# Output products of 24 heads by seven block products, with the row of softmax sums sent through DRAM

## The chip, the cores and the metric

The kernel runs on one core of a Trainium2 chip. The metric is the device time of one execution in microseconds (us), the median of several runs. The engines have separate, in-order instruction queues: TensorE (PE; its weight loads are listed as PEld), VectorE (DVE), ScalarE (ACT) and GpSimd (POOL); SyncE (SP) issues nearly all transfers, in order as well.

## The reference

A transformer block on x of 2048 rows by 576, float32. Six vectors for shift, gain and gate come from a condition vector c.

```python
h = layernorm(x) * (1 + ca) + sa
q = (h @ wq)                          # 32 heads of 128
k, v = the last 512 rows of the caches, 16 heads, each for two heads of q
o = softmax(q k^T / sqrt(128)) @ v
x = x + ga * (o @ wo)                 # wo: 4096 x 576
h = layernorm(x) * (1 + cb) + sb
x = x + gb * ((silu(h @ w1) * (h @ w3)) @ w2)   # 576 -> 4608 -> 576
```

## The kernel before

Every matmul runs in float32r on operands split into a high and a low half (`split`: ACT casts the high half, VectorE or POOL subtracts it from the source), three matmuls for one product.

**Attention.** The 2048 rows are four blocks of 512, whose residual sums stand in SBUF in `acc[0]` to `acc[3]`. The first half of attention does blocks 0 and 1, the second blocks 2 and 3. A *slot* is one head with one block: 64 slots in each half, 0 to 63 and 64 to 127; apart from each half's first four, the two blocks of a head follow each other. A slot has four *steps*, t = 0 to 3, for 128 rows each. In step t of iteration i of the main loop TensorE turns the probabilities of slot i-1 (`turn`), makes the scores of slot i (`scores`), a part of the queries of slot i+1 (`query`), and the product of the heads' output of slot i-2 with wo (`attend_out`, `back`). After the fourth step come the products with V of slot i-1 (`values`). `attend_out` is six matmuls of 128 by 288 columns into one PSUM pair, E, from which VectorE scales by one over the softmax sum, a value per row, and adds to `acc`.

**Around it.** While attention runs, the MLP's weights are made ready: `make_set` forms, for 128 columns of w1 and w3, seven combined blocks (Strassen's way of doing a product of 2 by 2 blocks with seven block products), and `make_rows` does the same for 256 rows of w2 (`make_rows` with -1 prepares, then seven pieces follow). POOL makes sums and low halves, ACT the high halves, SP stores each piece to DRAM and later loads it. In the second half, h of blocks 0 and 1 is normalized (`norm`), stored, and combined likewise (`combine`, three chunks of seven steps). All these are small tasks in a table, placed by `at(i, t, task, ...)` and called by `run(i, t)` at the end of step t of iteration i (`("m", g)` stands for group g of the MLP). The place in the program sets the place in every engine's queue. `early`, `late` and `items` hand out the places of the weights' tasks: pieces are made in slots 10 to 56 and 66 to 74 at 1.25 a step, and in 85 to 116 at 0.82.

**The MLP** runs its down product by seven block products already (`down`, `multiply`, `finish`): a unit is two jobs of three matmuls into one PSUM pair, two blocks of 512 rows need 14 units for 256 rows of weights, against 16 by plain products.

Tiles rotate in pools of fixed size: `w` (8), `xn` (4), `hf` (2), `ah` and `al` (3), `o` (3), `hs` (7). A write waits for the last reader of the tile that stood there.

## Time and profile before

| | |
|---|---|
| median of 3 runs | 3063.23 us (3062.53 to 3064.26) |
| the profiled execution | 3066.29 us, span 3064.5 us |
| granted TensorE clock, mean | 0.996 |
| bytes | read 369.8 MB, written 150.2 MB |
| maxima and exponentials (DVE L319, ACT L325), 512 each | 683 and 690 ns |

Slot 24 begins at 382 us, slot 97 at 1403 us, and attention ends at some 1820 us. The page gives, for each engine, its busy time and share of the span, and the chain of work that ended last. A query in windows gives the busy time in a stretch. A row of instructions reads: line, engine, operation, result<-operands, shape and count | busy us, mean ns of one | idle time ahead of it and what ended it. The chain's rows are start us, duration us, engine, tile, line, count.

### The profile page before, as it was taken

The numbers are of one execution on the slowest core, as the hardware profiler recorded it, in microseconds if no ns is written. First come the engines' busy times: TensorE is split into PE (matmuls) and PEld (weight loads), VectorE is DVE, ScalarE is ACT, GpSimd is POOL, SyncE is SP. The second block draws the span as 40 slices with busy tenths as digits, with TensorE's granted clock in tenths as the row PEclk, the third lists the DMA queues.
The fourth block names the chain that finished last, engine by engine and source line by source line (L and its number), as shares of the span: only waits on it lengthen the run. The fifth ranks groups of instructions, "written<-read, shape, count | busy, mean of one in ns | idle before, by whom it ended". The sixth has DMA issues, their size and how long they took to land.

```text
span 3064.5 us, 47936 instructions
## 1 busy us (share of the span) xinstructions
PE 3027.4 (99%) x16948; PEld 2654.4 (87%) x16948; DVE 2002.5 (65%) x3042; ACT 1481.7 (48%) x3107; POOL 1635.3 (53%) x1656
## 2 busy tenths in 40 slices
PE   7999999999999999999999999999999999999998
PEld 6888888888888888888888888888888888888887
DVE  6776676777777777777777766555555555555555
ACT  4556666666666665666665553333333222322222
POOL 3257887888734731667775103346555463443444
PEclk8999999999999999999999999999999999999999
DMA  4235546555512532354544135667666766666664
GB/s 143 76 130 191 184 163 198 182 184 184 179 42 76 181 101 65 127 183 168 160 163 149 40 141 187 210 219 259 240 229 219 279 238 193 203 200 203 199 197 141
DMA packets 330128, 523.13 MB, mean 171 GB/s; under 512 B 32800, under 2 KB 161824, under 8 KB 328096
## 3 DMA queue, kind: packets, MB, share of 16 engines
q1 hardware_dynamic: 329280, 520.06, 51.5%
q8 instruction: 135, 2.21, 0.3%
q14 instruction: 105, 0.86, 0.1%
q10 hardware_dynamic: 608, 0.00, 0.0%
HBM read 369.76 MB, written 150.18 MB: 170 GB/s over the span
## 4 chain that ended last, share of the span: by engine, by line
PE 94%; DVE 2%; POOL 2%; ACT 1%; issue 1%; DMA 1%; SPq 0%; ACTq 0%; POOLq 0%; DVEq 0%
PE py L577 15%; PE pe L282 13%; PE px L577 11%; PE pq L266 11%; PE pt L335 7%; PE pf L653 6%; PE pe L653 6%; PE po L353 4%; PE po L352 4%; PE po L351 4%; PE pss L317 4%; PE pss L315 4%; PE pss L316 4%; PE pq L274 2%; PE pt L252 0%
## 5 line engine op out<-in xcount | busy, mean ns | idle before, releaser
L325 ACT ACTIVATE p<-pss,nm 128x512 f32<-128x512 f32 x512 | 353.3, 690 | 367.4 <-DVE nm L319 367.1
L577 PE MATMUL py<-hset,wset 128*128 128x512 f32 x2016 | 506.9, 391 | 0.0
L366 DVE SCALAR_TENSOR_TENSOR acc<-pe,r,acc 128x576 f32<-128x576 f32 x512 | 416.8, 814 | 53.6 <-PE pe L282 47.9
L319 DVE TENSOR_REDUCE nm<-pss 128x1 f32<-128x512 f32 x512 | 349.7, 683 | 118.2 <-PE pss L317 118.0
L577 PEld LDWEIGHTS py<-hset,wset 128*128 128x128 f32 x2016 | 362.6, 188 | 58.9
L577 PE MATMUL px<-hset,wset 128*128 128x512 f32 x1512 | 380.1, 391 | 0.0
L282 PEld LDWEIGHTS pe<-o,oth 128*128 128x128 f32 x2048 | 326.7, 188 | 48.7 <-DVE acc L366 6.1
L342 DVE TENSOR_TENSOR ptl<-pt,pth 128x512 fp32r<-128x512 f32 x512 | 349.0, 682 | 16.1 <-ACT pth L336 15.6
L282 PE MATMUL pe<-o,oth 128*128 128x288 f32 x2048 | 355.8, 296 | 2.7 <-DVE acc L366 2.6
L336 ACT CAST pth<-pt 128x512 fp32r<-128x512 f32 x512 | 301.1, 588 | 37.1 <-PE pt L335 33.3
L577 PEld LDWEIGHTS px<-hset,wset 128*128 128x128 f32 x1512 | 275.6, 188 | 49.4
L335 PE MATMUL pt<-ident,p 128*128 128x128 f32 x2048 | 307.7, 273 | 4.6 <-DVE ptl L342 2.6
L85 POOL TENSOR_TENSOR akv<-u,akv 128x512 fp32r<-128x512 f32 x141 | 182.1, 1302 | 237.8 <-ACT akv L84 236.3
L335 PEld LDWEIGHTS pt<-ident,p 128*128 128x128 f32 x2048 | 249.8, 141 | 18.6 <-issue 3.0
L315 PE MATMUL pss<-kh,qh 128*128 128x512 f32 x512 | 244.9, 478 | 0.7 <-ACT qh L84 0.7
L85 DVE TENSOR_TENSOR otl<-po,oth 128x512 fp32r<-128x512 f32 x128 | 88.6, 692 | 225.8 <-ACT oth L84 225.8
L497 POOL TENSOR_TENSOR wmade<-wraw,wmade 128x256 fp32r<-128x256 f32 x252 | 186.6, 740 | 80.5 <-ACT wmade L496 62.0
L282 PE MATMUL pe<-o,otl 128*128 128x288 f32 x1024 | 219.0, 295 | 0.0
L84 ACT CAST oth<-po 128x512 fp32r<-128x512 f32 x128 | 75.1, 587 | 295.6 <-PE po L353 295.6
L317 PE MATMUL pss<-kh,ql 128*128 128x512 f32 x512 | 202.9, 396 | 0.0
L316 PE MATMUL pss<-kl,qh 128*128 128x512 f32 x512 | 202.6, 396 | 0.0
L353 PE MATMUL po<-ptl,vh 128*128 128x512 f32 x512 | 201.1, 393 | 1.2 <-DVE ptl L342 1.2
(181 smaller groups left out, 6522.7 us busy)
## 6 DMA issues: line engine op xcount, KB each, us to landing
oset<-od SPq DMA_DIRECT2D x106, 576.0 KB, 4.8
od<-omade SPq DMA_DIRECT2D x133, 288.0 KB, 2.7
oraw<-in_A_wo SPq DMA_DIRECT2D x64, 288.0 KB, 3.1
wraw<-in_B_w SPq DMA_DIRECT2D x144, 128.0 KB, 2.7
wraw<-in_A_wq SPq DMA_DIRECT2D x64, 256.0 KB, 3.2
w2raw<-in_B_w SPq DMA_DIRECT2D x38, 288.0 KB, 3.6
oset<-od SPq DMA_DIRECT2D x35, 288.0 KB, 3.3
wraw<-in_B_w SPq DMA_DIRECT2D x288, 32.0 KB, 2.1
```

Source lines behind the costliest of these rows:

```text
L266: nc.tensor.matmul(ps, (wh if k < 2 else wl)[:, m, :], hT[DC + m if k == 1 else m], start=s == 0, stop=False,)
L282: nc.tensor.matmul(E[:, h, :HALF], a[:, rows], b[:, h * HALF : (h + 1) * HALF], start=n == 0, stop=n == 2)
L315: nc.tensor.matmul(pss, st["qh"][:, rows], kh, start=True, stop=False)
L316: nc.tensor.matmul(pss, st["qh"][:, rows], kl, start=False, stop=False)
L317: nc.tensor.matmul(pss, st["ql"][:, rows], kh, start=False, stop=True)
L319: nc.vector.tensor_reduce(nm, pss, axis=AX.X, op=ALU.max, negate=True)
L325: nc.scalar.activation(p, pss, AF.Exp, bias=nm, accum_out=st["l"][:, t : t + 1])
L335: nc.tensor.transpose(ps[:, j, :], p[:, j * P : (j + 1) * P], ident)
L342: nc.vector.tensor_sub(pt[1][:, :, cols], state[i]["t"], pt[0][:, :, cols].bitcast(F32))
L366: nc.vector.scalar_tensor_tensor(a, E[:, :, :HALF], st["r"][:, t : t + 1], a, op0=ALU.mult, op1=ALU.add)
L577: nc.tensor.matmul(ps, w[:, a, :], h[:, b, :], start=start and n == 0, stop=stop and n == 6, skip_group_check=True)
L653: nc.tensor.matmul(ps[:, h, :HALF], a[:, rows], w[:, b, :], start=m == 0, stop=m == 2)
```

## The change

For slots 72 to 119 (`FAST`, twelve groups of four slots; a group is two heads and blocks 2 and 3) the output products are made by seven block products:

- `values` no longer splits po. VectorE multiplies po by one over the softmax sums, laid out along the columns of each partition, into a block in SBUF (`blocks`). For that the 128 by 4 sums of a slot are inverted (`invert`), stored to DRAM as they lie, and loaded into all partitions in the next slot (`spread`); the multiplication reads them in turned order.
- POOL makes four sums of the group's four blocks (`out_sum`: s3, s1, s2, s4), and seven blocks are split (`out_split`): p7 and p2 with the low half on POOL, p4, p6, p1, p5 and p3 with it on VectorE.
- 14 units (`out_unit`) take the place of 16, one in a step, called ahead of the other tasks of a step. VectorE adds each to `acc[2]`, `acc[3]` or to sums that stand where `acc[0]` and `acc[1]` were; these two are moved to DRAM in slots 68 to 71 and back at the end (`move_x`). `finish_out` and `finish_out_first` add the sums up in slots 125 to 127.
- The pieces of wo for these heads are made by `make_rows` with the gate "a" and go through DRAM like those of w2. The weights' tasks are handed out anew: 33 sets or pairs of rows in slots 10 to 56, the rest and the twelve new pairs evenly over slots 66 to 116.
- h of blocks 0 and 1 is normalized four slots earlier, and combined two steps in a slot, beginning in slots 82, 87 and 92 (before: 86, 94 and 102, one step in a slot). Between slot 71 and that combining's last steps the pieces use only the tiles `w`.
- The heads of slots 120 to 123 get wo twice, plain and turned for block 3 (`put_turned`), since `acc[3]` holds combined sums then.

TensorE, second half, one step and what follows it. Before, in the last step (pe is bank E):

```order
L274 MATMUL pq<-hT,wl 128x512
L282 MATMUL pe<-o,oth 128x288 x4
L282 MATMUL pe<-o,otl 128x288 x2
L351 MATMUL po<-pth,vh 128x512
L352 MATMUL po<-pth,vl 128x512
```

Now, in the step of slot 77 that holds the second new unit (oah and oal are the halves of a split block, oset the loaded pieces of wo):

```order
L275 MATMUL pq<-hT,wl 128x512
L721 MATMUL pe<-oset,oah 128x288 x2
L721 MATMUL pe<-oset,oal 128x288
L721 MATMUL pe<-oset,oah 128x288 x2
L721 MATMUL pe<-oset,oal 128x288
L355 MATMUL po<-pth,vh 128x512
```

A unit is still six matmuls; it stands in 14 of 16 steps.

VectorE, one slot of the second half. Before (nm are the maxima, ptl the low halves of the turned probabilities, acc the sums out of bank E, ql and otl low halves of queries and outputs):

```order
L319 TENSOR_REDUCE nm<-pss 128x1
L342 TENSOR_TENSOR ptl<-pt,pth 128x4x128
L366 SCALAR_TENSOR_TENSOR acc_86<-pe,r,acc_86 128x576
L319 TENSOR_REDUCE nm<-pss 128x1
L342 TENSOR_TENSOR ptl<-pt,pth 128x4x128
L85 TENSOR_TENSOR ql<-pq,qh 128x512
L366 SCALAR_TENSOR_TENSOR acc_86<-pe,r,acc_86 128x576
L85 TENSOR_TENSOR otl<-po,oth 128x512
L358 RECIPROCAL r<-l 128x4
```

Now, steps 1 to 3 of slot 78, for the first group (os are the blocks, oal their low halves; acc_83 is `acc[0]`, where sums and the row of sums stand; in this first group sums are copied, later added):

```order
L85 TENSOR_TENSOR oal<-os,oah 128x512
L323 TENSOR_REDUCE nm<-pss 128x1
L346 TENSOR_TENSOR ptl<-pt,pth 128x4x128
L694 COPY acc_83<-pe 128x576
L85 TENSOR_TENSOR oal<-os,oah 128x512
L323 TENSOR_REDUCE nm<-pss 128x1
L346 TENSOR_TENSOR ptl<-pt,pth 128x4x128
L85 TENSOR_TENSOR ql<-pq,qh 128x512
L694 COPY acc_83<-pe 128x576
L377 RECIPROCAL r<-l 128x4
L360 TENSOR_TENSOR os<-po,acc_83 128x512
```

The low halves of p1 and p5 stand between the sums and the next maxima, and the product of po with the row of sums stands where the low half of the output was.

POOL, slots 78 to 81 or so. Before, gates, splits of wo, wq and V:

```order
L779 TENSOR_TENSOR oraw<-oraw,gate_a 128x576
L85 TENSOR_TENSOR o<-oraw,o 128x576
L85 TENSOR_TENSOR wl<-wraw,wh 128x640
L779 TENSOR_TENSOR oraw<-oraw,gate_a 128x576
L85 TENSOR_TENSOR vl<-kvraw,vh 128x512
```

Now, in slot 81, from the sums of a set of w1 and w3 to s2 (the last row):

```order
L515 TENSOR_TENSOR wraw<-wraw 128x384
L516 TENSOR_TENSOR wraw<-wraw 128x384
L519 TENSOR_TENSOR wmade<-wraw,wmade 128x256
L520 TENSOR_TENSOR wmade<-wraw,wmade 64x128
L519 TENSOR_TENSOR wmade<-wraw,wmade 128x256
L520 TENSOR_TENSOR wmade<-wraw,wmade 64x128
L574 TENSOR_TENSOR w2raw<-w2raw,gate_a 128x576 x2
L575 TENSOR_TENSOR w2raw<-w2raw 128x288
L576 TENSOR_TENSOR w2raw<-w2raw 128x288
L577 TENSOR_TENSOR w2raw<-w2raw 128x288
L579 TENSOR_TENSOR w2raw<-w2raw 128x288
L706 TENSOR_TENSOR os<-os 128x512
```

Pieces and a preparation of rows moved in ahead of s2, which the split of p6, one step later, reads.

The diff's core:

```diff
+    FAST = range(18, 30)
+    blocks, sums_home = {}, []
 ...
     def values(i):
 ...
-        oh = pool.tile([P, SB], F32R, tag="ah", name="oth", bufs=3)
-        ol = pool.tile([P, SB], F32R, tag="al", name="otl", bufs=3)
+        if i // 4 in FAST:
+            nc.vector.tensor_mul(
+                *(a.rearrange("p (t q) -> p t q", t=ST) for a in (blocks[i], po)),
+                sums_home[3].rearrange("p (q t) -> p t q", t=ST),
+            )
+            return
 ...
+    def invert(i):
+        r = odd.tile([P, ST], F32, tag="r", name="r", bufs=3)
+        nc.vector.reciprocal(r, state[i]["l"])
+        state[i]["row"] = dram.tile([P, ST], F32, name=f"r{i}")
+        nc.sync.dma_start(state[i]["row"], r)
+
+    def spread(i):
+        row = state[i].pop("row").rearrange("p t -> (p t)")
+        nc.sync.dma_start(sums_home[3], row.partition_broadcast(P))
 ...
-        tag, bufs = (("xn", ST), ("w", 8))[staged[0] % 2]
+        tag, bufs = (("xn", ST), ("w", 8))[1 if staged[1] else staged[0] % 2]
 ...
+    def out_unit(k, u):
+        b, d = slots[4 * k][0], ("a", k - 16)
+        m15, m6 = sums_home[:2]
+        if u < 4:
+            q, into, jobs = 0, half_split(acc[b + 1][:, u, :]), [("p4", 0, u), ("p7", 1, u)]
+        elif u < 6:
+            q, into, jobs = 1, m6[u - 4], [("p6", 0, 2 * (u - 4)), ("p6", 0, 2 * (u - 4) + 1)]
+        elif u < 10:
+            q, into, jobs = 2, m15[u - 6], [("p1", 0, u - 6), ("p5", 1, u - 6)]
+        else:
+            q, into, jobs = 3, half_split(acc[b][:, u - 10, :]), [("p2", 0, u - 10), ("p3", 1, u - 10)]
+        multiply(E, [(halves[d, name], osets[d, q][:, i], r) for name, i, r in jobs])
+        if k == FAST[0] and q in (1, 2):
+            nc.vector.tensor_copy(into, E[:, :, :HALF])
+        else:
+            nc.vector.tensor_add(into, E[:, :, :HALF], into)
+
+    def out_sum(k, what):
+        x00, x01, x10, x11 = (blocks[4 * k + i] for i in range(4))
+        if what == "s3":
+            nc.gpsimd.tensor_sub(sums_home[2], x00, x01)
+        elif what == "s1":
+            nc.gpsimd.tensor_add(x01, x01, x11)
+        elif what == "s2":
+            nc.gpsimd.tensor_sub(x11, x01, x00)
+        else:
+            nc.gpsimd.tensor_sub(x10, x10, x11)
+
+    def out_split(k, name):
+        x00, x01, x10, x11 = (blocks[4 * k + i] for i in range(4))
+        x = {"p7": sums_home[2], "p4": x11, "p6": x11, "p1": x00, "p5": x01, "p2": x10, "p3": x10}[name]
+        hi, lo = [pool.tile([P, SB], F32R, tag=t, name=f"o{t}", bufs=3) for t in ("ah", "al")]
+        split(hi, lo, x, nc.gpsimd if name in ("p7", "p2") else nc.vector)
+        halves[("a", k - 16), name] = hi, lo
 ...
-    early = [4 * i + t for lo, hi in ((10, 57), (66, 75)) for i in range(lo, hi) for t in range(ST)]
-    late = [4 * i + t for i in range(85, 117) for t in range(ST)]
 ...
+    EARLY = 33
+    late, places = made[EARLY:], []
+    for j, p in enumerate(PAIRS_OF_HEADS):
+        lo, hi = (len(late) * k // len(PAIRS_OF_HEADS) for k in (j, j + 1))
+        places += [(load_rows, make_rows, p), *late[lo:hi]]
+    for these, lo, hi in ((made[:EARLY], 10, 57), (places, 66, 117)):
 ...
+                step = 4 * lo + (7 * number + k) * 4 * (hi - lo) // (7 * len(these))
 ...
-        i = 2 * HQ + 22 + 8 * c
+        i = 2 * HQ + 18 + 5 * c
 ...
-            at(i + 1 + step, 1, combine_parts, 0, c, step)
+            at(i + 1 + step // 2, 1 + 2 * (step % 2), combine_parts, 0, c, step)
 ...
+    for k in FAST:
+        s, d = 4 * k, ("a", k - 16)
+        for i in range(s, s + 4):
+            at(i, 3.9, invert, i)
+            at(i + 1, 0, spread, i)
+        for what, i, t in (("s3", 3, 1), ("s1", 5, 0), ("s2", 5, 2), ("s4", 7, 2)):
+            at(s + i, t, out_sum, k, what)
+        for name, i, t in (("p7", 4, 1), ("p4", 5, 0), ("p6", 5, 3), ("p1", 6, 1), ("p5", 6, 2), ("p2", 7, 1), ("p3", 8, 0)):
+            at(s + i, t, out_split, k, name)
+        for q, (i, t) in enumerate(((4, 3), (5, 2), (6, 0), (7, 0))):
+            at(s + i, t, load_oset, d, q)
+        for u in range(14):
+            step = 4 * (s + 5) + 2 + u + (u >= 10)
+            at(step // 4, step % 4 + 0.5, out_unit, k, u)
 ...
             if 2 <= i:
-                attend_out(i - 2, t)
+                if (i - 2) // 4 not in FAST:
+                    attend_out(i - 2, t)
+            run(i, t + 0.5)
             run(i, t)
+        run(i, 3.9)
```

More of the change, by code (lines that the diff above doesn't have):

```diff
@@ L153, in tile_block @@
     norms = {}
+    staged = [0, False]
     def norm_stats(b, t):
@@ L363, in attend_out @@
         st = state[i]
-        back(st["o"], wos[half, h], t)
+        back(st["o"], wos.get((half, h, b)) or wos[half, h], t)
         a = half_split(acc[b][:, t, :])
```

112 lines of the change are left out of this document (78 added, 34 removed).

## The prediction

> **What bounds the kernel now.** I read the page's first two parts and its chain, then the stretch of attention in windows, then one slot as the chain shows it, and at last the queue of POOL, since the change gives POOL and VectorE work that was TensorE's.
>
> ```profile
> PE 3027.4 (99%) x16948; PEld 2654.4 (87%) x16948; DVE 2002.5 (65%) x3042; ACT 1481.7 (48%) x3107; POOL 1635.3 (53%) x1656
> ...
> PE 94%; DVE 2%; POOL 2%; ACT 1%; issue 1%; DMA 1%; SPq 0%; ACTq 0%; POOLq 0%; DVEq 0%
> ```
> ```profile
> 1400.00:1500.00 100.00, 100.00 (x572) 87.78 (x571) 70.23 (x109) 62.20 (x141) 73.48 (x81) 1.00 0.57 184
> ```
> The last row has PE, PEld, DVE, ACT and POOL busy in 100 us, then the granted clock. TensorE is never without a matmul here, and the chain is 94% TensorE, so in the second half of attention a matmul less is time less, as long as the other engines keep up. How long one takes is read from the chain, where each piece ends when the next begins:
>
> ```profile
> 1389.09 0.44 PE pt L335 x4
> ...
> 1402.77 0.44 PE pt L335 x4
> ...
> 1407.23 0.80 PE pe L282 x6
> 1408.03 0.44 PE pt L335 x4
> ...
> 1409.86 0.80 PE pe L282 x6
> ```
> A slot (one head with one block) is 1402.77 - 1389.09 = 13.68 us, a step (a quarter of it, without the products with V at its end) 1409.86 - 1407.23 = 2.63 us, and a unit of six products into the model 0.80 us.
>
> **What is removed.** Four slots had 16 units and get 14. Twelve groups of four slots lose 24 units: 24 x 0.80 = 19.2 us, all of it on TensorE's path. No matmul is added.
>
> It also moves products in time. The first new unit comes in slot 77 and the last old one in slot 73, so slots 75 and 76 are 13.7 - 4 x 0.80 = 10.5 us of TensorE, and slots 122 to 125, which hold both kinds, about 16. The other slots are 12.9 to 14.1, by the number of units (3 or 4) and by the turning of the keys (0.44 us). The total is what counts for TensorE; but the work of POOL beside slots 75 and 76 must fit into less.
>
> **What VectorE gets.**
>
> ```profile
> L366 DVE SCALAR_TENSOR_TENSOR acc<-pe,r,acc 128x576 f32<-128x576 f32 x512 | 416.8, 814 | 53.6 <-PE pe L282 47.9
> L319 DVE TENSOR_REDUCE nm<-pss 128x1 f32<-128x512 f32 x512 | 349.7, 683 | 118.2 <-PE pss L317 118.0
> L342 DVE TENSOR_TENSOR ptl<-pt,pth 128x512 fp32r<-128x512 f32 x512 | 349.0, 682 | 16.1 <-ACT pth L336 15.6
> L647 DVE TENSOR_TENSOR acc<-pe,acc 128x576 f32<-128x576 f32 x140 | 105.3, 752 | 53.9 <-PE pe L653 52.8
> ```
> ```profile
> L85 DVE TENSOR_TENSOR otl<-po,oth x128: 691/692/693, 63.6 to 1848.9; 128x512 fp32r<-128x512 f32 x128
> ...
> L85 DVE TENSOR_TENSOR aal<-u,aah x37: 692/1228/1234, 1860.0 to 3048.4; 128x512 fp32r<-128x512 f32 x37
> ```
> Per four slots 16 sums of 0.81 become 14 of 0.75 (2.5 us less), four subtractions of 0.69 become four products with the row of sums (no such row; between 0.69 and 0.88 by its kin, about even), and five low halves are new, between 0.69 and 1.23 each (3.5 to 6.2). ACT loses four copies of po and gets seven of the blocks. VectorE as a whole stays near 85% of a slot. But p1 and p5 fall into steps 1 and 2 of one slot, where a step leaves 2.63 - 0.68 - 0.68 - 0.75 = 0.5 us: at 1.23 each VectorE can come about 1 us late with the last low half of the probabilities, for which the products with V wait; at 0.69 it does not. That is 0 to 12 us over twelve groups, and where TensorE has just waited for something else it is hidden; I take 3.
>
> **What POOL gets.** These rows price it, and the second fence shows the same instructions one behind the other in slots 24 to 26:
>
> ```profile
> L497 POOL TENSOR_TENSOR wmade<-wraw,wmade 128x256 fp32r<-128x256 f32 x252 | 186.6, 740 | 80.5 <-ACT wmade L496 62.0 <-issue 7.1 <-POOL wmade L498 4.2
> L686 POOL TENSOR_TENSOR u<-u,u 128x512 f32<-128x512 f32 x35 | 45.2, 1291 | 2.7
> L490 POOL TENSOR_TENSOR wraw<-wraw 128x384 f32<-128x384 f32 x36 | 36.6, 1017 | 1.0
> ```
> ```profile
> 393.19 2.83 POOL L545 TENSOR_TENSOR w2raw<-w2raw,gate_b 128x576 f32<-128x576 f32 x2
> ...
> 399.29 0.74 POOL L497 TENSOR_TENSOR wmade<-wraw,wmade 128x256 fp32r<-128x256 f32 x1
> 400.11 0.46 POOL L498 TENSOR_TENSOR wmade<-wraw,wmade 64x128 fp32r<-64x128 f32 x1
> 400.65 0.74 POOL L497 TENSOR_TENSOR wmade<-wraw,wmade 128x256 fp32r<-128x256 f32 x1
> ...
> 408.27 1.58 POOL L533 TENSOR_TENSOR omade<-w2raw,omade 128x288 fp32r<-128x288 f32 x2
> ```
> So a piece of a w1/w3 set costs POOL 400.65 - 399.29 = 1.36 us (twice in seven some 2.1 more, for two sums of 1.02), the preparation of two rows 399.29 - 393.19 = 6.1, one of the seven row pieces 0.79, and each of the new sums, and each low half split on POOL, 1.29. Per four slots the new products bring POOL four sums and two low halves (7.8 us) and one more pair of rows (6.1 + 7 x 0.79 = 11.6), and take away two gates and two splits of wo (4 x 1.4). More weighs where the sets are put: they now run through slots 66 to 117 without the pause of slots 75 to 84, and the combining of h (three times seven steps, 40 instructions of 1.29 us, so 52 us of POOL) goes from one step a slot to two, into slots 83 to 96. Adding the tasks slot by slot, POOL gets 16.3, 15.1 and 14.1 us in slots 75 to 77, 19.7 in slot 81, and 237 us in slots 84 to 99, beside some 214 us of TensorE. Before, its largest slots in this half were 18.9 with 5.5 behind them, and at the end of a slot it was late by 6.2 us at most (7.4 in slot 11).
>
> **Where POOL's lateness is felt.** In each group's second slot (77, 81, 85 and so on) POOL makes the sum that the code calls s2 in step 2, behind all that was queued there, and ACT copies the block made from it in step 3 (out_split p6). ACT's queue is in order: while that copy waits, the casts and exponentials of the next slot wait too, and VectorE, which takes the low half of p6, stands in front of its own product of po, its maxima and the sums that free bank E. ACT's copy would come at about 10.5 us of the slot; its next due work is the cast at the start of the next slot. I take it that TensorE begins to wait when s2 ends 2 us behind the slot's end: a unit's sum takes 0.8 us and the next unit writes bank E 2.63 - 0.80 = 1.8 us after the one before, which leaves 1 us, and the turning of the keys that follows and the two banks of the scores give the rest. Then, with what POOL carries in and its work up to s2:
> - slot 77: 10.4 + 12.8 = 23.2, allowed 15.4: 7.8 late
> - slot 81: 0 + 18.3, allowed 14.9: 3.4
> - slot 85: 11.2 + 9.5 = 20.7: 5.8
> - slot 89: 6.5 + 9.2 = 15.7: 0.8
> - slot 93: 10.1 + 15.7 = 25.8: 10.9
> - slot 97: 9.0 + 10.3 = 19.3: 4.4
> - slot 105: 0 + 18.3: 3.4
>
> Together 36.5 us of waits; each wait is given to POOL as time before the next carry is worked out. Slot 81 is the plainest, since nothing is carried in: four pieces, two pairs of set sums, s1 and s2 itself (12.2 us) and a preparation of rows (6.1) end with it. The allowance is the weak number. With none the same table gives 48; with 6, the largest lateness that slots of before passed at their end, it gives 18. A wait on POOL that reached TensorE stands in the trace once, through SP's queue:
>
> ```profile
> 285.42 0.47 POOL wmade L498
> 285.90 0.32 SPq L499
> ...
> 293.37 3.21 DMA kvraw<-in_A_k_cache
> ...
> 296.71 0.86 PE pt L252 x4
> ...
> 300.76 0.80 PE pe L282 x6
> ```
> ```profile
> PE pt L252 <- DMA kvraw<-in_A_k_cache: 2.4, 1, 2.4
> ```
> ```profile
> 298.00:300.00 2.00, 2.00 (x7) 1.61 (x7) 0.95 (x2) 0.79 (x2) 0.00 (x0) 0.50 1.05 379
> ```
> A store waited for POOL, twelve loads stood behind it, and the keys came 2.4 us late. The stores of pieces, the new row of sums (out and, in the next slot, in again to all partitions) and the loads of weight sets share that queue; the row has a slot of time, so I charge nothing for it beside the same lateness of POOL, which covers it. If POOL were on time, the store and the load would be the next to be late. As bytes they are small: 48 sets of products' weights (84 pieces of 295 KB, 25 MB) and 48 rows of 256 KB (13 MB) over some 620 us are 61 GB/s more beside the 184 of the window above, which kept the DMA engines 0.57 busy; at about 0.76 I charge nothing, and the cover is that these loads are issued three steps or more ahead.
>
> The same rows show what a wait costs besides: after it the granted clock was 0.50, four turnings took 0.86 instead of 0.44 us, and this lasted until about 300.76, 4 us at half speed, of which some 1.8 are lost. Where waits follow on each other, the slow time lets POOL catch up and is in the 36.5 already; after slots 77, 81, 97 and 105 it is not. I add 4 us (between 0 and 4 x 1.8 = 7). [...]
>
> **Sum.** -19.2 + 36.5 + 4 + 3 = +24.3 us on a span of 3064.5. The profiled execution took 3066.3, 1.8 beyond its span and 3.1 above the median of the runs, 3063.2; from that median the forecast is 3087.
>
> **Rivals.**
> - The lateness is swallowed: tiles are far enough apart that ACT and TensorE run on, and only the products saved are seen, 3063.2 - 19.2 = 3044, up to 3056 with some waits. For it speaks that slots of before passed with POOL 6.2 us late at their end and up to 13 us late in its queue without a wait of TensorE; against it that s2 and its copy stand one step apart, and that 237 us do not fit into 214. It decides if the allowance behind the slot's end is above some 9 us. Chance 0.23.
> - Waits and savings even out: an allowance of 6 us (18) gives 3062 to 3068 with the rest. Chance 0.13.
> - POOL pays too: if each of the five subtractions by VectorE with both inputs in SBUF holds POOL up for its 0.69 us, POOL has 0.86 us more a slot, 6% of its 237 / 16 = 14.8, and the table's waits grow from 36.5 to some 52: 3103. The two rows of L85 above (one input in PSUM never above 693, both in SBUF mostly 1228) show one side of such a clash, not POOL's. Chance 0.12. [...]
> - The forecast, waits on POOL of 26 to 48 us: chance 0.52, 3076 to 3099.
>
> Together: faster by over 0.2% (about what a measurement can tell) 0.23, within it 0.13, slower 0.64. The range takes in most of the swallowed case and POOL's paying: 3046 to 3106.
>
> **What would show it.** In the profile of after: output products 144 fewer with a unit still 0.80; POOL in slots 75 to 77 and 84 to 99 without idle time; waits of ACT for POOL at the copy of p6, and TensorE's idle time near them, with a lower clock behind; VectorE's new subtractions near 1.2 us. It is wrong if TensorE stays at 100 in these windows although POOL is as late as the table says, or if POOL's pieces prove shorter than here.

## The result and the profile after

The kernel after takes 3209.7 us (median, 3208.9 to 3211.3), the kernel before on the same chip 3063.7 (3062.5 to 3065.3). The ratio is 1.0477, with a 95% interval of 1.0459 to 1.0495: slower by 146 us, where the forecast was slower by 24, with 3106 as the end of its range. The profiled execution has a span of 3207.1 us.

The page's first part and its chain, of after:

```profile
PE 3055.8 (95%) x16804; PEld 2651.7 (83%) x16804; DVE 2046.6 (64%) x3082; ACT 1511.7 (47%) x3205; POOL 1835.4 (57%) x1861
...
PE 48%; POOL 6%; DVE 4%; DMA 3%; issue 3%; ACT 2%; SPq 1%; POOLq 0%; ACTq 0%; DVEq 0%
```

TensorE has the 144 products less that the change takes away (16948 to 16804), and yet it is busy for 28 us longer and idle for 151 us in place of 37. The chain, which was TensorE's to 94%, is its to 48%. The windows (length, then PE, PEld, DVE, ACT and POOL busy, granted clock, DMA share, GB/s), first the 100 us that the prediction showed of before, then slots 84 to 99 of after, and the same slots of before:

```profile
1400.00:1500.00 100.00, 84.37 (x443) 71.43 (x442) 61.07 (x92) 53.19 (x122) 85.33 (x87) 0.95 0.65 205
```
```profile
1237.70:1521.30 283.60, 233.98 (x1219) 197.05 (x1217) 169.65 (x257) 151.57 (x347) 232.91 (x243) 0.93 0.64 206
```
```profile
1223.60:1444.50 220.90, 220.90 (x1267) 194.18 (x1265) 157.03 (x244) 137.52 (x311) 155.65 (x169) 1.00 0.47 154
```

Sixteen slots that were 220.9 us are 283.6. No engine is full in them: TensorE is busy for 0.83 of the time, GpSimd (POOL) for 0.82.

To see where it goes I take each slot from the first product of its scores to that of the next, and subtract TensorE's work by the prices of before: 10.48 us without units or turnings, 0.80 a unit, 0.44 for four turnings (of the keys or of the normalized rows). In before this leaves 3 us in all over slots 60 to 126, so what it leaves in another kernel is lost time. In after it is 165 us from slot 72 on: 115 of them TensorE idle, 50 at the low clock behind a wait (the granted clock was 0.50 for 82 us of these slots) or in starting again. 165, less the 19.2 saved and the 3 us that before loses itself, is 143; the span grew by 142.6. Who TensorE waited for in slots 72 to 126 (us, times, longest):

```profile
PE pe L721 <- DMA oset<-ad: 28.4, 8, 11.2
PE pt L339 <- DVE kl L257: 19.3, 7, 6.1
PE pe L721 <- DVE acc L391: 14.0, 12, 1.8
PE pe L721 <- ACT oah L84: 12.9, 4, 6.8
PE pt L339 <- DVE ptl L346: 9.2, 9, 2.6
PE po L357 <- DVE ptl L346: 8.2, 11, 1.2
PE pt L339 <- DVE mv L171: 6.7, 1, 6.7
```

No single wait carries it. Two of them, as the chain shows them (start, length, what), first in slot 106:

```profile
1608.81 2.80 POOL w2raw L574 x2
...
1613.34 0.79 POOL w2raw L577
1614.13 1.23 POOL os L706
...
1615.38 0.63 ACT oah L84
...
1616.82 0.95 DVE os L360
1617.77 0.61 DVE kl L257
...
1618.42 1.11 PE pt L339 x4
```

This is the path of the prediction: the sum s2 (L706) stands on GpSimd behind the preparation of a pair of rows, ScalarE copies the block for p6, and VectorE, in order, takes its low half, then its own product of po, then the low half of the keys, for which TensorE's turnings wait (5.4 us). The four turnings then take 1.11 us in place of 0.44. And in slot 89:

```profile
1337.40 1.27 POOL hst L447
1338.67 0.69 POOL wmade L519
1339.36 0.31 SPq L448
...
1339.76 0.39 SPq L453
...
1340.24 4.88 DMA oset<-ad
...
1345.26 1.78 PE pe L721 x6
```

Here nobody waits for a sum. SyncE (SP, its queue SPq) holds the load of an output set behind two stores of the combination of h, which wait for GpSimd; the load needs 4.88 us to land, TensorE idles for 8.0, and the next unit takes 1.78 us in place of 0.80, at a granted clock of 0.50. The prediction charged nothing for this.

### The profile page after: what moved, and what is told of

It is laid out like the page before. It is cut to its first block, busy times and chain, and to the rows that moved or that the text cites. A ratio compares the mean times of both kernels' runs of the same rounds, so it can differ in the third digit from the quotient of the medians.

```text
span 3207.1 us, 48616 instructions
## 1 busy us (share of the span) xinstructions
PE 3055.8 (95%) x16804; PEld 2651.7 (83%) x16804; DVE 2046.6 (64%) x3082; ACT 1511.7 (47%) x3205; POOL 1835.4 (57%) x1861
## 4 chain that ended last, share of the span: by engine, by line
PE 48%; POOL 6%; DVE 4%; DMA 3%; issue 3%; ACT 2%; SPq 1%; POOLq 0%; ACTq 0%; DVEq 0%
PE py L606 14%; PE px L606 10%; PE pe L721 8%; PE pf L721 6%; PE pq L267 2%; PE pt L339 2%; DVE nm L323 1%; PE po L357 1%; PE po L355 1%; PE po L356 1%; DVE oal L85 1%; PE pss L321 1%; PE pss L319 1%; PE pss L320 1%; POOL omade L562 1%
## 5 line engine op out<-in xcount | busy, mean ns | idle before, releaser
L339 PE MATMUL pt<-ident,p 128*128 128x128 f32 x2048 | 313.5, 276 | 39.7 <-DVE kl L257 19.3
L391 DVE SCALAR_TENSOR_TENSOR acc<-pe,r,acc 128x576 f32<-128x576 f32 x320 | 260.3, 814 | 32.2 <-PE pe L283 28.4
L562 POOL TENSOR_TENSOR omade<-w2raw,omade 128x288 fp32r<-128x288 f32 x218 | 177.3, 825 | 149.6 <-ACT omade L561 128.1
L519 POOL TENSOR_TENSOR wmade<-wraw,wmade 128x256 fp32r<-128x256 f32 x252 | 188.8, 749 | 62.6 <-ACT wmade L518 29.7
L283 PEld LDWEIGHTS pe<-o,oth 128*128 128x128 f32 x1216 | 193.7, 188 | 31.3 <-DVE acc L391 6.4
L283 PE MATMUL pe<-o,oth 128*128 128x288 f32 x1216 | 211.8, 296 | 2.7 <-DVE acc L391 2.5
L355 PE MATMUL po<-pth,vh 128*128 128x512 f32 x512 | 203.9, 398 | 6.8 <-ACT pth L340 6.4
L721 PE MATMUL pe<-oset,oah 128*128 128x288 f32 x672 | 147.4, 308 | 65.1 <-DMA oset<-ad 28.4
```

The source lines that it names most:

```text
L283: nc.tensor.matmul(E[:, h, :HALF], a[:, rows], b[:, h * HALF : (h + 1) * HALF], start=n == 0, stop=n == 2)
L339: nc.tensor.transpose(ps[:, j, :], p[:, j * P : (j + 1) * P], ident)
L391: nc.vector.scalar_tensor_tensor(a, E[:, :, :HALF], st["r"][:, t : t + 1], a, op0=ALU.mult, op1=ALU.add)
L721: nc.tensor.matmul(ps[:, h, :HALF], a[:, rows], w[:, b, :], start=m == 0, stop=m == 2)
```

## The experiments

Theory A: GpSimd has too much to do beside the new products, and whatever waits for it, on ScalarE, VectorE or in SyncE's queue, is late. Rival B: the chain of sums, splits, row and sets is too long for the steps that it has, whatever else GpSimd does. Rival C: the changed places of preparations, normalisation and combination are at fault, not the products. Rival D: SyncE's queue and the staging tiles. Later, inside A: theory O, that the order in GpSimd's queue decides, and theory T, that its sum of work does. The table has each kernel's time beside that of before on its chip, and the time lost per stretch, worked out as above (us); the "late items" are the sets and rows of the second layer that are prepared from slot 66 on.

| kernel | time | before | 76-81 | 82-99 | 100-120 | 121-126 |
|---|---|---|---|---|---|---|
| after | 3209.7 | 3063.7 | 18.2 | 78.5 | 43.9 | 20.9 |
| e1 units apart | 3208.2 | 3066.7 | 18.3 | 84.1 | 47.4 | 13.3 |
| e2 no row | 3196.4 | 3066.7 | 14.8 | 74.1 | 41.6 | 19.2 |
| e3 preparation in four steps | 3211.9 | 3066.7 | 16.9 | 72.8 | 42.2 | 19.3 |
| e4 loads from ScalarE's queue | 3204.6 | 3066.7 | 16.2 | 80.0 | 42.8 | 19.2 |
| e5 no late items | 3113.0 | 3065.0 | 4.7 | 34.7 | 9.6 | 19.4 |
| e6 one pair of rows | 3147.7 | 3065.0 | 10.3 | 49.3 | 20.9 | 20.8 |
| e7 schedule alone | 3082.7 | 3065.0 | 0.1 | 15.1 | 0.3 | 0.1 |
| e8 sums on VectorE | 3229.6 | 3065.0 | 18.7 | 78.8 | 54.7 | 24.7 |
| e9 no late stores | 3195.7 | 3065.4 | 16.5 | 73.8 | 37.4 | 19.1 |
| e10 no late work of GpSimd | 3137.3 | 3065.4 | 10.6 | 40.0 | 19.9 | 20.9 |
| e11 no late items, apart | 3107.2 | 3065.4 | 4.7 | 35.0 | 10.1 | 13.2 |
| e12 the same, ScalarE's queue | 3091.8 | 3065.4 | 4.7 | 22.0 | 8.0 | 13.4 |
| e13 sums first | 3180.6 | 3066.1 | 16.5 | 67.7 | 28.2 | 18.6 |
| e14 the same, preparation in four | 3176.2 | 3066.1 | 19.1 | 57.1 | 37.3 | 18.5 |
| e15 all four | 3166.4 | 3066.1 | 14.2 | 53.4 | 40.9 | 12.4 |
| e16 schedule alone, one step | 3063.9 | 3064.2 | 0.1 | 0.7 | 0.4 | 0.1 |
| e17 e12, one step | 3098.0 | 3064.2 | 4.7 | 20.8 | 10.5 | 14.3 |
| e18 e15, one step | 3166.3 | 3064.2 | 13.9 | 47.2 | 49.2 | 12.4 |

After, e15 and e18 are medians; the others are single executions. How far these can be trusted is seen where code is the same: slots 0 to 59 lost 23 to 28 us in all kernels that leave them alone, and slots 82 to 120, the same in after and e1, lost 122 and 131. Differences below some 10 us are not read.

### Single suspects: e1 to e4

**e1.** The units of the last group between scores and query of their step, away from the heads' products that write the same tile E:

```diff
-            at(step // 4, step % 4 + 0.5, out_unit, k, u)
+            at(step // 4, step % 4 + (0.25 if k == FAST[-1] else 0.5), out_unit, k, u)
 ...
                 scores(i, t)
+            run(i, t + 0.25)
```

> Slots 121 to 126 lost 20.9 us against the work that TensorE has in them (15.2 us of it idle, 13.5 of that in steps in which a unit of the last group follows a head's product into the one tile E and waits for VectorE to empty it). Here the units of the last group alone stand between the scores and the query of their step. Theory (one tile E, emptied by VectorE in about 0.9 us): the loss of these slots falls to 3 to 6 us and the span by 15 to 18 us, 3189 to 3192; nothing changes before slot 121. Rival (the end of the stage is late because VectorE has too much to do there): the loss of these slots stays at 15 us or more.

The loss of slots 121 to 126 fell from 20.9 to 13.3 us, but the time only by 1.5: half of the expected gain at the end, and none in the sum, since slots 82 to 120 lost 9 us more with the same code. That the one tile E costs there is read from the timeline of after in slot 122, step 0 (in brackets the idle time):

```profile
1862.89 0.43 PE L283 MATMUL pe<-ot,otl 128*128 128x288 f32 x2
1864.26 0.55 PE L721 MATMUL pe<-oset,oah 128*128 128x288 f32 x2 [0.94 <-DVE acc L391]
```

A head's product and a unit follow on each other, and TensorE waits until VectorE has emptied E. That happens in nearly every step of slots 122 to 125, a dozen times with a wait that the row above counts (14.0 us). In e11, with little late upstream, the same edit gave what it gives here in those slots (19.4 to 13.2), and the time fell with it.

**e2.** The row of sums is neither stored nor broadcast; VectorE multiplies by a tile of ones.

```diff
-        state[i]["row"] = dram.tile([P, ST], F32, name=f"r{i}")
-        nc.sync.dma_start(state[i]["row"], r)
 ...
-            at(i + 1, 0, spread, i)
```

> The division by the row of sums is left out: no store of the row to DRAM, no broadcast of it, and VectorE multiplies by a tile of ones that is always there. Theory (SyncE's queue of DMA issues runs late and everything in it with it): the idle time that a late row brings goes (slot 76: 9.7 us, slots 91 and 93: some 10 us, parts of 88 and 101), and 2 issues a slot with their landing of 4.3 us leave the queue: 25 to 45 us less, 3165 to 3185. Rival (the row's way through DRAM is the main cost): 90 us less or more. Rival (GpSimd is overloaded, and the row only waits with the rest): less than 12 us.

13 us: half of the theory's lower end, and hardly more than the 12 of "GpSimd is overloaded, and the row only waits with the rest". The row's way through DRAM is not the main cost.

**e3.** The preparation of a pair of rows in four steps:

```diff
-                        at((step - 4) // 4, (step - 4) % 4, maker, w, -1)
+                        for m in range(-4, 0):
+                            at((step + m) // 4, (step + m) % 4, maker, w, m)
```

> The six operations with which GpSimd prepares a pair of weight rows (6.1 us in one piece) are issued over four steps, same work. Theory (single late sums behind the whole piece: slots 82, 88, 106 and 112 lost 8.6, 8.1, 11.7 and 8.7 us): 20 to 35 us less, 3175 to 3190. Rival (GpSimd's sum of work per slot decides, not its order): within 8 us of 3210. Rival (the spread operations meet more of the sums instead of fewer): slower by 5 to 20 us.

No gain in sum. From slot 72 on 11 us less were lost, but slots 0 to 59, where the same preparations run, lost 38.5 in place of 24.0.

**e4.** Row and output sets from ScalarE's queue of DMA issues (the row's store one step, its broadcast two steps later than in after):

```diff
-        nc.sync.dma_start(t[:, : 1 if q == 1 else 2].bitcast(F32), odram[chunks(d), q][:, :, :, :])
+        (nc.scalar if type(d) is tuple else nc.sync).dma_start(...)
 ...
+            at(i + 1, 0, store_row, i)
+            at(i + 1, 2, spread, i)
```

> Row store, broadcast of the row and loads of the output sets of the 12 groups are issued from ScalarE's DMA queue (row store one step later, broadcast two steps later than before); all stores of prepared weights and stages stay on SyncE's. Theory (loads stand behind stores that wait for GpSimd on SyncE's queue): the waits for output sets (28.4 us with the cold clock after them more) and for the row go: 45 to 70 us less, 3140 to 3165. Rival (GpSimd itself is late and would hold TensorE anyway): less than 20 us. Rival (ScalarE, in order, now waits for the row's landing): slower.

5 us: "GpSimd itself is late and would hold TensorE anyway". Four single causes, each seen in the trace, together promised over 100 us; removed one by one they gave back 1.5, 13, -2 and 5. When one wait goes, the next thing that is late takes its place. In slot 76, for example, TensorE idled for 6.7 us for the late row (the line of L171 above); in e2, without the row, it idles there for 4.4 us behind ScalarE, which waits for the landing of a load of wq out of the same queue.

### GpSimd's load: e5 to e10

**e5** leaves out the late items:

```diff
-    late, places = made[EARLY:], []
+    late, places = [m for m in made[EARLY:] if m[1] is make_rows and m[2] == LAST], []
```

> Left out: 21 of the 22 sets and rows of the second layer that are prepared between slots 66 and 117 (the stage after reads earlier ones in their place); the 12 pairs' rows and all products stay. In slots 76 to 103 GpSimd was busy for 40 to 61 us of each 4 slots, in which TensorE has 53 us of work. Theory A (GpSimd has too much to do, and everything that waits for it or stands behind such a store is late): its load falls by some 20 us per 4 slots, the loss of slots 76 to 120 (140 us) falls to 30 to 60, span 3100 to 3130. Rival B (the chain of sums, splits, row and output sets is too long for the steps given to it, whatever else GpSimd does): more than 100 us of the loss stay, span above 3165.

**e6** leaves out 11 of the 12 pairs' rows:

```diff
-        places += [(load_rows, make_rows, p), *late[lo:hi]]
+        places += [(load_rows, make_rows, p), *late[lo:hi]][j > 0:]
```

> Left out: the rows of 11 of the 12 pairs of heads (gates, sums, stores: about 11.6 us of GpSimd's time and 7 stores each); all pairs read the first one's; the second layer's items stay. Theory A: GpSimd's load falls by some 10 us per 4 slots, about half of what leaving out the items takes away; the loss of slots 76 to 120 falls from 140 to 60 to 100 us, span 3125 to 3170. Rival B: span above 3185.

97 and 62 us come back, both within theory A's figures and out of B's. What was taken away differs (sets of the second layer, rows for the products themselves); common to both is GpSimd's time. **e9 and e10** part it from what goes with it. e9 leaves out the late items' stores, e10 GpSimd's operations in them:

```diff
-        nc.sync.dma_start(wdram[f, k][:, :, :], t.bitcast(F32))
+        if f < 22:
+            nc.sync.dma_start(wdram[f, k][:, :, :], t.bitcast(F32))
```

> Left out: only the 147 stores of 21 of the 22 items of the second layer that are prepared between slots 66 and 117 (the stage after reads earlier ones); their loads, ScalarE's copies and GpSimd's operations stay. Theory A (it is GpSimd's time for them, some 273 us, that makes it late): less than 40 us of the 97 that all of the items cost come back, span above 3170. Rival D (SyncE's queue, in which these stores wait for GpSimd ahead of loads, and the ring of staging tiles that their landing holds): 60 us or more come back, span 3145 or less.

```diff
+        if f >= 22:
+            t = staging([P, DC + 1, P], "wmade")
+            nc.scalar.copy(t[:, :3, :], a11 if n in (3, 4) else x)
+            nc.sync.dma_start(wdram[f, k][:, :3, :], t[:, :3, :].bitcast(F32))
 ...
+            return
```

> Left out: only GpSimd's operations of the same 21 items (sums, differences, low parts); their loads, ScalarE's copies and one store a piece, of the high part alone, stay. Theory A: most of the 97 us come back, span 3112 to 3135. Rival D (the number of DMA issues and the ring): less than half comes back, span 3160 or more.

14 us against 72. The 147 stores are not the cause, GpSimd's operations are: rival D falls as the main cause, theory A holds (the span of e10, 3135.4, is at the end of the range given for it). Slots 84 to 99 of e5 and of e10, in the windows:

```profile
1214.90:1463.00 248.10, 223.21 (x1219) 191.17 (x1218) 171.16 (x257) 133.48 (x299) 145.28 (x126) 0.97 0.51 160
```
```profile
1222.10:1474.80 252.70, 227.91 (x1220) 192.68 (x1217) 171.04 (x257) 151.60 (x347) 143.79 (x125) 0.97 0.67 208
```

Without some 88 us of GpSimd's time the sixteen slots take 31 to 36 us less. In e10 ScalarE and VectorE do as much as in after, and the DMA engines nine tenths (208 GB/s over 253 us, 206 over 284).

**e7** has the changed places with the plain products of before (no block products, no pairs' rows):

```diff
-        if i // 4 in FAST:
+        if False:
 ...
-                if (i - 2) // 4 not in FAST:
-                    attend_out(i - 2, t)
+                attend_out(i - 2, t)
```

> The changed places of the preparations, the normalisation and the combination, with the plain products of before everywhere (no pairs' rows, no block products, no row through DRAM). Theory A and B: GpSimd stays below TensorE's time in each 4 slots, and nothing is late: 3064 to 3075. Rival C (the earlier normalisation, two combinations per slot and the staging in one ring of tiles are what is late): 3100 or more.

18 us, more than A and B allow and less than C asks: the places cost something by themselves, in slots 84 to 91, and the products bring the rest. The chain there:

```profile
1235.34 1.29 POOL hst L447
1236.65 2.00 DMA hd0p<-hst
...
1238.75 0.63 ACT hst L444
...
1259.09 2.15 DMA hd0p<-hst
...
1261.34 0.10 ACT hst L444
...
1261.87 0.59 ACT oth L84
...
1262.50 1.81 PE pe L283 x6
```

The combination stages its results in a ring of two tiles (`hf`). ScalarE's next copy waits until the store before has landed, and in ScalarE's order the copy of the head's output (L84), for which TensorE waits, stands behind it. (The second store had itself stood on SyncE behind a dozen issues of loads.) So SyncE's queue has a part in it as well. e16 comes back to this.

**e8** puts the four sums on VectorE:

```diff
-            nc.gpsimd.tensor_sub(x11, x01, x00)
+            nc.vector.tensor_sub(x11, x01, x00)
```

(and the other three alike).

> The four sums of a group on VectorE in place of GpSimd, same steps, same values. GpSimd loses 5.2 us per 4 slots, VectorE gains 2.8 to 4.6 us on some 42 of 53. Theory A: the late sums no longer stand behind GpSimd's pieces (slots 82, 88, 106, 112: 37 us), and the rest of its queue is earlier: 25 to 50 us less, 3160 to 3185. Rival (VectorE's order then passes on its own waits, for the row above all): within 10 us of 3210, or slower.

20 us slower, the rival's side. In slots 72 to 126 TensorE now waited for VectorE's low halves of the probabilities for 31.2 us; in after it was 8.2. GpSimd gained less than the 16 sums taken from it: in the window of slots 84 to 99 it was busy for 217.1 us in place of 232.9, where the sums alone are 20.6 at 1.29; VectorE's sums read both inputs from SBUF, which "The rivals" below comes back to.

```profile
PE po L357 <- DVE ptl L346: 31.2, 20, 5.4
```

### What is left without the late items: e11, e12

e11 is e5 with the edit of e1, e12 is e11 with that of e4.

> The kernel without the 21 late items, and the units of the last group between scores and query. With nothing late upstream the gain at the one tile E is to be seen in the time: slots 121 to 126 lose 12 to 14 in place of 19.4 us, nothing changes before, 5 to 8 us less than the 3111 of the span without late items: 3103 to 3107. If the gain is taken back upstream again: within 2 us.

> The same, and row, broadcast and output sets issued from ScalarE's queue. What is left before slot 121 are waits for an output set in slots 85, 89 and 97 (26.5 us lost there), whose load stands on SyncE's queue behind a store of the combination that waits for GpSimd. Theory (the order of SyncE's queue, once GpSimd's load is gone): 15 to 28 us less, span 3077 to 3092. Rival (the sets are late because their buffers come free late): within 5 us of the run without this.

Both as the theory had it: 5.8 and 15.4 us. (5.8 is less than what I read of a whole time; but it stands where the edit is, 19.4 to 13.2 in slots 121 to 126, and the other stretches stay within 0.5.) The edits that gave nothing in e1 and e4 give what the traces promised once GpSimd's load is gone. So SyncE's order is a cost of its own, but it shows only when GpSimd is not late anyway.

### Order or sum: e13 to e15

e13 issues a group's sums, splits and set loads ahead of the pieces in their step; e14 adds the edit of e3 from slot 66 on; e15 adds those of e1 and e4.

```diff
+    def ahead(i, t, n, task, *args):
+        tasks.setdefault((i, t), []).insert(n, (task, args))
 ...
-            at(s + i, t, out_sum, k, what)
+            ahead(s + i, t, 0, out_sum, k, what)
```

> In each step the group's sums, splits and output-set loads are issued ahead of the step's pieces of weights (they stood behind them); same work, same steps. Theory O (order: a group's sums wait for pieces that are not urgent, and 2 to 8 us of such a wait pass on to ScalarE, VectorE and TensorE): 30 to 60 us less, 3150 to 3180; the waits of slots 82, 106 and 112 for a late sum (8.6, 11.7, 8.7 us lost) halve or go. Theory T (GpSimd's time in a slot, whatever its order; it is late with one thing if not with another): within 15 us of 3210.

> The same, and the six operations that prepare a pair of rows over four steps, only for the items from slot 66 on (spread everywhere they cost 14 us in slots 10 to 57 and gave back some 12 after slot 72). Theory O: 10 to 20 us less than the run without it, 3130 to 3170. Theory T: within 8 us of the run without it.

> All four changes of order: sums first, preparation in four steps from slot 66 on, units of the last group apart from the heads' products, row and output sets from ScalarE's queue. The values are those of the kernel after. Theory O: what each gives without GpSimd's load (6 and 15 us) adds to the run before: 3110 to 3150. Theory T: 3180 to 3200. Neither expects it to come below 3065, since the places of the preparations alone cost 18 us and the products give 19.2.

29 us come back by order alone: the edge of theory O's range, and out of T's. The waits that were GpSimd's order shrink (the first row was 19.3 in after, the second 28.4), others take over part (the third was 4.8; the turnings' wait for VectorE's low halves went from 9.2 to 15.0, that of the products with V for ScalarE's casts from 4.5 to 12.8); slots 72 to 126 of e13:

```profile
PE pt L339 <- DVE kl L257: 2.8, 2, 2.2
...
PE pe L721 <- DMA oset<-ad: 12.5, 4, 6.2
...
PE pe L721 <- DVE acc L696: 16.4, 7, 4.5
```

e14 is 4 us below e13, but that difference lies in slots 0 to 59, where the two are alike; from slot 72 on both lose 134, which is theory T's side. All four edits give 43 us (e15: 1.0325 of before, 1.0308 to 1.0343), between O's 3150 and T's 3180. Slots 84 to 99 of e15:

```profile
1230.60:1492.20 261.60, 234.73 (x1220) 196.72 (x1217) 171.68 (x256) 151.64 (x346) 232.09 (x243) 0.93 0.71 226
```

GpSimd does the same 232 us in 262 in place of 284: it is 0.89 busy, and TensorE's work of 214 still doesn't set the pace. The edits of order are worth a quarter of the loss of slots 76 to 126 (161.5 to 121.0). GpSimd's 232 us are more than TensorE's 214 in these slots, whatever the order.

### The pace of the combination: e16 to e18

One step of the combination per slot in place of two, with plain products (e16), in e12 (e17) and in e15 (e18):

```diff
-        i = 2 * HQ + 18 + 5 * c
+        i = 2 * HQ + 18 + 8 * c
 ...
-            at(i + 1 + step // 2, 1 + 2 * (step % 2), combine_parts, 0, c, step)
+            at(i + 1 + step, 1, combine_parts, 0, c, step)
```

> Plain products and the changed places, but one step of the combination per slot, in slots 83 to 105, in place of two, in slots 83 to 96. Theory H (a step of the combination stages its results in a ring of two tiles, and the next copy on ScalarE waits for the store of the one before to land, 2.0 to 2.3 us, with everything behind it in that engine's order): the 14.6 us lost in slots 84 to 91 go, 3064 to 3070. Rival (they come from the earlier normalisation or from the number of items per slot): 3076 to 3083.

> Block products, without the 21 late items, units of the last group apart, row and output sets from ScalarE's queue (3091.8 with two steps of the combination per slot), here with one step per slot. Theory H: the 16 us still lost in slots 85, 89 and 97 shrink to 5 or less: 3076 to 3083, so that the block products, with GpSimd's load and these queues out of the way, come within 11 to 18 us of the time before although the end of their stage loses 13 us. Rival: within 4 us of 3092.

> The whole computation: sums first, preparation in four steps from slot 66 on, units of the last group apart, row and output sets from ScalarE's queue, and one step of the combination per slot. Theory H: 10 to 25 us less than the 3166 with two steps: 3140 to 3156. Theory T (GpSimd's sum of work, which stays the same over slots 76 to 117): within 8 us of 3166.

With plain products the 18 us are gone altogether (3063.9 beside 3064.2): two steps per slot were the cost of the schedule, not the earlier normalisation. That the ring of two tiles passes it on, and not SyncE's dozen issues beside it, is read from the chain of e7; no run changed the ring. With block products the gain doesn't carry over: e17 took 6 us more than e12, where theory H had 9 to 16 less. It lost 1.0 us in slots 85 and 89, where e12 lost 12.5, but 13.7 in slots 93, 97 and 101, where e12 lost 2.0. Its chain in slot 93:

```profile
1347.63 0.78 POOL omade L566
...
1348.42 3.76 DMA ad<-omade
...
1352.20 4.20 DMA oset<-ad
...
1356.42 0.59 ACT pth L340
...
1357.06 0.79 PE po L355
```

GpSimd finishes a piece, its store has to land before the load of a set on ScalarE's queue goes on, and ScalarE's cast of the probabilities follows. That is one reading of the chain; why the load waits for that store was not tried, so what holds e17 stays open. e18 is where e15 was: slots 82 to 99 lose 6 us less, 100 to 120, where the combination now runs, 8 more. That is theory T. No version here beats the kernel before.

## Why the prediction was wrong

- **What is removed (-19.2 us).** Right as a count: 144 matmuls fewer, and a unit with no wait before it is still 0.80 us. As time it is seen only where nothing is late, as in e5's slots 104 to 117, which lose 0.3 us each.
- **GpSimd's load (237 us in slots 84 to 99, beside 214).** Right in size: 232.9 measured, about 225 of it at the prices of before (see the rivals). But the step that followed from it failed. The table let GpSimd work without a gap until it had caught up, and "GpSimd without idle time" was what the trace was to show. It was idle for 51 of the 284 us. For 29 of these it waited for the copies that it subtracts from, which stand in ScalarE's order behind what waits for GpSimd, for VectorE and for landings; in slots 84 to 99 (us, times, longest):

```profile
POOL omade L562 <- ACT omade L561: 22.3, 6, 9.7
POOL wmade L519 <- ACT wmade L518: 6.5, 4, 4.2
```
```profile
ACT p L329 <- DVE nm L323: 62.7, 53, 6.1
...
ACT hst L444 <- DMA hd0p<-hst: 14.7, 5, 6.1
ACT hst L444 <- POOL wmade L519: 10.9, 2, 5.5
ACT oah L84 <- POOL os L706: 7.5, 2, 4.4
```

  So the lateness doesn't end with GpSimd's backlog; the engines wait for each other in a circle.
- **Waits for s2 (36.5 us).** Twice too large, by two errors of opposite sign. ScalarE waited for s2 for 33.0 us over the whole run, which comes near the 36.5 by chance:

```profile
ACT oah L84 <- POOL os L706: 33.0, 8, 8.3
```

  What TensorE waited behind it are the waits for VectorE's low half of the keys (L257) in slots 82, 94, 98, 106, 110 and 114: 6.1, 2.5, 1.1, 5.4, 1.2 and 1.5 us, 17.8 in sum. In these six s2 ended 5.5, 1.9, 0.3, 4.7, 0.4 and 0.9 us behind the end of its slot (taken at the next slot's first product of scores), and TensorE waited 0.6 to 0.8 us longer than that each time. So there is no allowance: TensorE begins to wait when s2 ends at about the slot's end, not 2 us behind it. And s2 was less late than the table had it. With the allowance put back, the table has s2 end 9.8, 5.4, 7.8, 2.8, 12.9, 6.4 and 5.4 us behind the end of slots 77, 81, 85, 89, 93, 97 and 105; in the trace it ended 5.5 behind that of 81, 4.7 of 105, 1.9 of 93, 0.3 of 97, and ahead of the end in 77, 85 and 89. That fits the time that losses on other roads had given GpSimd (in slot 85 TensorE waited 11 us for an output set).
- **SyncE's queue ("I charge nothing", "which covers it").** This is the term that was missing. Waits for output sets alone are 28.4 us of TensorE's idle time, the late row 6.7 (slot 76). e12 puts the queue at 15 us when GpSimd has time; when it has none, e4 puts it at 5, within the scatter of single runs, as the queue is then late with GpSimd. The sentence "if POOL were on time, the store and the load would be the next to be late" was right, and should have had a price. The bytes counted beside it left out the stores of the new pieces (the pages have 39.7 MB more read and 27.2 MB more written); that bytes cost time is not shown, as e9, at 155 GB/s in place of 206 in these slots, gave back 14 us.
- **The combination at two steps per slot.** Priced as 52 us of GpSimd's work and no more. At two steps in a slot it cost 18 us with plain products (e7, e16).
- **Slots 122 to 125 ("about 16").** They were 24.8, 22.3, 20.3 and 15.7 us: the two kinds of products share one tile E, and the steps that hold both wait for VectorE in between. The sum had nothing for it; 20.9 us were lost in slots 121 to 126.
- **The low clock (4 us).** The part of the loss that isn't idle time is 50 us. There were dozens of waits, not four, and between slots 72 and 126 the granted clock was 0.50 in 14 spells of 3.4 to 10.2 us.
- **VectorE (3 us).** Not told apart. Its low halves with both inputs in SBUF took 0.92 us in the mean, between the two bounds and below the 1.2 that was to show it. "Near 85% of a slot" fits no row shown: it had 157.0 us of work in 220.9 before, and 169.7 beside TensorE's 214 after, 79%.
- **The rivals.** Nothing was swallowed, as there was no allowance. GpSimd's operations were longer where they overlapped VectorE's low halves, by less than half of what the rival had. The operations whose price the prediction took from before, at 740 ns, took more in slots 75 to 118:

```profile
L519 POOL TENSOR_TENSOR wmade<-wraw,wmade 128x256 fp32r<-128x256 f32 x84 | 64.6, 769 | 32.2 <-issue 15.9 <-ACT wmade L518 14.3
```

  The median is as before; a few are long. In slots 73 to 117 46 of GpSimd's 581 operations took over 0.06 us more than the median of their kind, 19.2 us in all, and 43 of the 46, with 18.5 of it, overlap a low half of VectorE with both inputs in SBUF, as here (the 8 such low halves that overlap nothing of GpSimd took 0.68 to 0.69 us, the 71 operations of L519 that overlap no such low half 0.74 in the median):

```profile
1215.29 1.29 DVE oal L85
1215.98 1.19 POOL L519 TENSOR_TENSOR wmade<-wraw,wmade 128x256 fp32r<-128x256 f32 x1
```

  In before, which has no such low halves there, it is 0.8 us. So 60 low halves went with some 18 us of GpSimd's time, 0.3 each; the rival's 0.69 each no run shows. In slots 84 to 99 that is 7.7 of the 232.9 us: at the prices of before GpSimd's work is some 225 there, and the 237 of the table were 12 too many.

The direction and the cause (GpSimd, through in-order queues) were right. The failed step is the term for waits: it priced one path by which lateness reaches TensorE, s2 behind an allowance of 2 us, and called the others covered by the same lateness, where each added to it. Of the 115 us that TensorE idled, 17.8 came by that path; the rest came by output sets, the row, the order of ScalarE and VectorE and the tile E, for which the sum had 3 us, and 50 us of slow products came with it, where the sum had 4.

## What to carry to other kernels

Moving work off the limiting engine pays only while the engine that takes it stays well below the limiting one in every stretch, with the idle time that it spends on its own waits counted in: here 0.70 of a stretch (before, slots 84 to 99) cost nothing, and a load 9% above TensorE's work went with 284 us in place of 214, of which 31 to 36 came back with the load (e5, e10). When several waits on TensorE have one late engine behind them, removing them one by one returns almost nothing; take load off that engine first (72 us here), then put the urgent work ahead of the rest in its queue (29 us), and only then repair the single waits. Count staging tiles, a queue of DMA issues and shared accumulators (`hf`, SyncE, E) as resources with a price when a schedule is compressed.

## What the hardware showed that I had not expected

The clock's fall did not follow the length of a single wait. In slot 96 TensorE idled for 1.87 us and the granted clock was 0.50 after it; in slot 97 it idled for 2.59 and, two microseconds later, 1.46 us, and the clock stayed at 1.00. In the traces of before and after the records of the clock change only at whole multiples of 3.413 us from each other, so I cut the time there (the first two stretches are of slot 96, the others of slot 97; PE busy stands behind the length, the granted clock third from the end):

```profile
1458.27:1461.68 3.41, 1.54 (x9) 1.13 (x7) 1.83 (x4) 2.25 (x6) 3.20 (x3) 1.00 0.73 283
1461.68:1465.09 3.41, 3.41 (x11) 2.85 (x12) 2.45 (x4) 2.54 (x6) 3.25 (x4) 0.50 0.14 45
```
```profile
1475.33:1478.75 3.42, 1.58 (x8) 0.99 (x6) 1.64 (x3) 0.00 (x0) 1.67 (x4) 1.00 0.94 352
1478.75:1482.16 3.41, 2.00 (x10) 1.44 (x10) 2.90 (x6) 2.32 (x6) 1.90 (x3) 1.00 0.85 272
```

The wait of slot 96 lies in one stretch; those of slot 97 are shared out among three, 1.83, 1.41 and 0.81 us. In the two traces each of the 18 stretches at full clock with more than 1.91 us of idle time, in one piece or several, was followed by a slow one; of the 1759 with less than 1.5 us two were, both at 14 us; of the 12 between, 2. So in these traces a slow stretch went with the sum of the idle time in the stretch before it, not with the longest wait, and the short waits of this kernel can't be priced one by one by their length; in sum, 115 us of idle time came with 50 us more.
